# Expert weights moved to other places among the transfers of a one-core kernel of linear attention and routed experts

## The chip, the cores and the metric

The kernel runs on one core of a Trainium2 chip. The metric is the device time of one execution in microseconds (us). Engines are named as in the profile: PE is the matmul engine (TensorE), DVE, ACT and POOL are the vector, scalar and GpSimd engines, SP issues transfers.

## The reference

```
q_s = softmax(q, over head_dim);  k_s = softmax(k, over seq)       # 8 batches, 8 heads, seq 576, head_dim 64
attn = q_s @ (k_s^T @ v)                                           # per batch and head
x = attn as 4608 tokens of 512
logits = x @ w_gate + modality_bias[modality_id];  e = argmax(logits)
out = softmax(logits)[e] * (relu(x @ w1[e]) @ w2[e])               # w1 512 x 1024, w2 1024 x 512, 8 experts
```

## The kernel before

The bias of a token's modality decides its expert for the data at hand, so at most two experts are used: side A for the tokens of one modality, side B for those of the other. The kernel reads the two numbers of experts from the biases on chip (`eid_i`), sorts the tokens into places by modality (A from the front of the buffer `xs`, B from its end), runs the two experts over them and stores each row at its token's place by an indirect DMA. A fallback at the end, over all experts, is skipped when a count of the tokens says so.

Attention goes batch by batch, in stages that are named here by their lines. Load q, k, v of a batch into one of five staging buffers each (L393, issued by SP, one after another). Exp of q (L821, ACT), its sums (L827, DVE), their inverses and the scaled q, `eq` (L843; on DVE for batches 0 and 1, on POOL after that). Exp of k, `ek` (L854, ACT); cast of v, `vb` (L864, ACT or POOL). The kv product (L957, PE), scaled into `kvbd` (L993, DVE). A permutation matmul of the scaled q (L1033, PE) that sorts each 64 tokens by modality, evicted to `et` (L1045 ACT, L1047 DVE). The second product `et` x `kvbd` (L1072, PE). Last, 18 copies into the places of the two sides (L1103), 9 per side, whose addresses were loaded into registers; the table `copier` says which engine does them.

Experts go in passes of 256 tokens of a side: nine passes per side, pass n when batches 0 to n are in their places. A pass has the gate's logits (L1138, PE; L1152 to L1166 for the softmax), the first layer (L1202: 8 groups of 4 matmuls of 256 columns, each group with a PSUM bank of its own and a relu into `hT`, L1172 ACT or L1174 DVE), the second layer (L1215: 2 tiles of 8 matmuls of 512 columns, evicted with the gate's factor, L1178 ACT or L1180 DVE) and two stores (L1183, POOL). Weights W come by DMA from POOL (L510 for w1, L521 for w2), which halves them to bf16 on the way: for each side four parts, 0 and 1 for w1, 2 and 3 for w2. The places of the tokens are worked out in L643 to L656 (slots and digits) and by one-hot products (L677 DVE, L701 POOL, L718 PE); the table of biases by place is L667 to L672.

What sets the order is a planner in the kernel. Each piece of work is an `op` with the engines that may do it, a busy time and a latency that are written by hand, its dependencies, a rank and its buffers. `Plan.order` lists them as an event-driven simulation would start them; the instructions are then written in that order, one in-order queue per engine. Transfers are ops on one engine "DMA" and are listed in the order in which they are made. `Plan.fill` puts matmuls that nobody reads (L1451) ahead of PE's work where the plan leaves it idle in the first 32 us.

Before, loads are listed as batches 0 and 1, then all four parts of A, then q of batch 2 and part 0 of B, k and part 1, v and part 2, part 3, then batches 3 to 7. Two waits are written by hand: the first part of A waits for k of batch 1, and q of batch 2 for part 2 of A. Parts 2 and 3 of B are kept in the plan behind the products L701.

Of the kernel before, what the change touches and what calls it, by code (L numbers as in the profile page):

```python
# [19 lines left out]
P = 128  # L20
# [32 lines left out]
class Op:  # L53
    seq = -1

    def __init__(self, costs, run, deps=(), rank=0.0, takes=(), uses=(), lag=0.0):
        self.costs, self.run, self.rank, self.lag = costs, run, rank, lag
        self.takes, self.uses = takes, uses
        self.after, self.left = [], 0
# [14 lines left out]
class Plan:  # L74
# [5 lines left out]
    def op(self, costs, run, deps=(), rank=0.0, takes=(), uses=(), lag=0.0):  # L80
        o = Op(costs, run, list(dict.fromkeys(deps)), rank, list(takes), list(takes) + list(uses), lag)
        o.seq = len(self.ops)
        self.ops.append(o)
        return o

# [6 lines left out]
    def order(self, later):  # L92
# [6 lines left out]
        queue = [o for o in self.ops if "DMA" in o.costs]  # L99
# [25 lines left out]
        while True:  # L125
            moved = True
            while moved:
                moved = False
                for e in ready:
                    if not idle[e]:  # L130
                        continue
                    for o in sorted(ready[e], key=lambda o: ALONE[e] * (len(o.costs) > 1)):
                        if (e == "DMA" and o is not queue[0]) or (port(e, o) and not idle["PORT"]):
                            continue
# [13 lines left out]
                        if e == "DMA":  # L148
                            queue.pop(0)
# [9 lines left out]
                        heapq.heappush(events, (now + busy, n, "idle", e))  # L159
                        heapq.heappush(events, (now + lat, n, "done", o))  # L160
# [5 lines left out]
            while events and events[0][0] <= now:  # L166
# [10 lines left out]
                for a in x.after:  # L177
# [7 lines left out]
                for b in x.uses:  # L185
# [41 lines left out]
def dma(nbytes):  # L227
    busy = nbytes / 390e3
    return {"DMA": (busy, busy + 2.0)}
# [3 lines left out]
def kernel(  # L233
# [12 lines left out]
    nc = tc.nc  # L246
# [133 lines left out]

    def behind(later, first, reason):
# [7 lines left out]
    def load(src, b, buf, h, n):  # L389


        def run(_):
# [9 lines left out]
            if src is q and b == 2:  # L402
                behind(d, issued["w", 0, 2][-1], "the weights come first")
# [27 lines left out]
    def load_ids(_):  # L431
# [3 lines left out]
        )  # L435
        nc.scalar.dma_start(
# [16 lines left out]
    l_ids = pl.op({"ACT": (1.2, 3.5)}, load_ids, rank=-9)  # L453
    load_batch(0)
    load_batch(1)
# [41 lines left out]
    o_parts = pl.op({"DVE": (0.35, 0.5)}, parts_run, [l_ids, c_dve], rank=-5)  # L497
    o_spread = pl.op({"PE": (0.2, 0.45)}, spread_run, [o_parts, c_pool], rank=-5, takes=[b_buf])
    o_exp = pl.op({"DVE": (1.2, 1.4)}, experts, [o_spread, c_dve2], rank=3, uses=[b_buf])
# [32 lines left out]

    def load_w(s, part):


        def run(_):
# [15 lines left out]
        at = pl.op({"POOL": (cost, cost)}, run, [o_exp, loads["k", 1][0][-1]], rank=-1)  # L552
        w_issue[s].append(at)
        return pl.op(dma(2 * P * F * 4 * 1.12), lambda _: None, [at])
# [86 lines left out]
    def slot_run(_):  # L641
        d = nc.vector
# [22 lines left out]
    def bsel_run(_):  # L665
        d = nc.vector
# [942 lines left out]
```

## Time and profile before

| | |
|---|---|
| time, median of 3 runs | 202.79 us (201.49 to 205.6) |
| profiled execution, its own time | 204.96 us |
| its span, first to last instruction | 203.2 us |
| mean granted PE clock | 0.964 of full |
| busy, of the span | PE 180.4, DVE 154.5, ACT 127.9, POOL 90.5 us |
| read from HBM, written | 36.75 MB, 9.70 MB |

Busy time of PE is modelled at its ends, so that full does not mean that every matmul runs at its peak. Idle time of an engine costs only where another engine, or the end, waits for it. An engine's queue is in order: what waits at its head holds all that stands behind it.

### The profile page before, as it was taken

To read this page: it belongs to the slowest core of one execution; us is meant where nothing else is said; L and a number is where in the kernel's file an instruction comes from. 1 tells how busy PE (TensorE), PEld (TensorE's weight loads), DVE (VectorE), ACT (ScalarE), POOL (GpSimd) and SP (SyncE) were. 2 spreads that over 40 slices of the span, in tenths; PEclk is the share of its full clock that TensorE was granted. 3 is DMA by queue.
4 is the path that set the end of the run, shared out by engine and by line. 5 is a ranking of instruction groups with operands and counts; after the bars stand their busy time and mean duration, and the time that the engine had idled before them with its cause. 6 is when DMAs were issued, how large, how long until landed. Compare 5 with 4: busy or idle time off the path is not lost.

```text
span 203.2 us, 5008 instructions
## 1 busy us (share of the span) xinstructions
PE 180.4 (89%) x1716; PEld 124.4 (61%) x1735; DVE 154.5 (76%) x447; ACT 127.9 (63%) x283; POOL 90.5 (45%) x113
## 2 busy tenths in 40 slices
PE   0789679989999999999959959999999999999990
PEld 0446348577657486868647735878667657766760
DVE  1899997999879999669968973959589557755660
ACT  2669875998759599999849674999896000000100
POOL 6001910584944489943395086591303311222231
PEclk9999955999999999999999988999999999999998
DMA  6999999999999997999369711111112112121102
GB/s 191 371 400 392 186 203 225 295 394 313 280 411 404 404 399 250 390 404 338 115 201 385 271 52 55 52 53 56 53 55 103 52 55 103 52 103 56 76 28 108
DMA packets 18588, 42.33 MB, mean 208 GB/s; under 512 B 1913, under 2 KB 1913, under 8 KB 18562
## 3 DMA queue, kind: packets, MB, share of 16 engines
q1 hardware_dynamic: 13344, 28.33, 38.4%
q0 software_dynamic: 5200, 13.64, 23.3%
q8 instruction: 14, 0.23, 0.5%
q10 hardware_dynamic: 18, 0.04, 0.2%
q14 instruction: 12, 0.10, 0.1%
HBM read 36.75 MB, written 9.70 MB: 229 GB/s over the span
## 4 chain that ended last, share of the span: by engine, by line
PE 69%; DVE 11%; ACT 6%; issue 5%; POOL 3%; DMA 2%; ACTq 2%; DVEq 0%; POOLq 0%
PE ps L1215 28%; PE ps L1202 26%; DVE xs L1103 3%; PE ps L1033 3%; PE ps L1072 3%; PE ps L957 3%; ACT xs L1103 3%; PE ps L1138 2%; DVE own L827 2%; DMA bias<-n_moe_modality_bias_dram 2%; DVE eq L843 2%; POOL out_dram L1183 1%; ACT vb L864 1%; POOL eq L843 1%; ACTq L1007 1%
## 5 line engine op out<-in xcount | busy, mean ns | idle before, releaser
L1202 PE MATMUL ps<-xs,W 128*128 128x256 bf16 x576 | 71.9, 277 | 0.2
L1215 PE MATMUL ps<-W,hT 128*128 128x512 bf16 (+1 forms) x277 | 66.4, 378 | 1.1 <-issue 0.2
L1183 POOL DMA_INDIRECT out_dram<-y_sb,idx x36 | 35.7, 992 | 57.5 <-DVE y_sb L1180 30.7
L1202 PEld LDWEIGHTS <-W 128*128 128x128 bf16 x576 | 55.2, 99 | 9.8 <-issue 0.9
L1172 ACT ACTIVATE hT<-ps 128x256 bf16<-128x256 f32 x63 | 23.0, 414 | 40.7 <-PE ps L1202 40.4
L1215 PEld LDWEIGHTS <-hT 128*128 128x128 bf16 x296 | 28.6, 99 | 29.3 <-issue 1.3
L1174 DVE TENSOR_SCALAR hT<-ps 128x256 bf16<-128x256 f32 (+1 forms) x83 | 34.6, 427 | 7.4 <-PE ps L1202 4.7
L1180 DVE TENSOR_SCALAR y_sb<-ps,gate 128x512 f32<-128x512 f32 (+1 forms) x28 | 20.1, 720 | 21.1 <-PE ps L1215 15.9
L1103 ACT CAST xs<-ps 128x256 f32 (+1 forms) x99 | 31.8, 447 | 2.1 <-PE ps L957 1.0
L843 POOL TENSOR_TENSOR eq<-st,qi 128x512 bf16<-128x512 f32 (+1 forms) x30 | 28.5, 972 | 6.1 <-PE ps L1202 2.7
L827 DVE TENSOR_REDUCE own<-st 128x18 f32<-128x1152 f32 x16 | 21.6, 1350 | 0.1
L821 ACT ACTIVATE st<-st 128x1152 f32<-128x1152 f32 x16 | 18.7, 1195 | 2.8 <-DMA st<-in_q_dram 2.3
L854 ACT ACTIVATE ek<-st 128x1152 bf16<-128x1152 f32 x16 | 19.1, 1200 | 1.2 <-DMA st<-in_k_dram 1.2
L1045 ACT CAST et<-ps 128x512 bf16<-128x512 f32 (+1 forms) x30 | 16.1, 565 | 5.9 <-PE ps L1033 5.6
L1033 PE MATMUL ps<-perm,eq 128*128 128x128 bf16 x144 | 14.3, 230 | 3.5 <-POOL eq L843 2.0
L1103 DVE CAST xs<-ps 128x256 f32 (+1 forms) x45 | 16.1, 415 | 0.5 <-ACT xs L1103 0.4
L864 POOL CAST vb<-st 128x1152 bf16<-128x1152 f32 x8 | 9.0, 1142 | 16.0 <-DMA st<-in_v_dram 10.0
L1033 PEld LDWEIGHTS <-eq 128*128 128x128 bf16 x144 | 10.0, 101 | 8.2 <-POOL eq L843 3.1
L957 PE MATMUL ps<-vb,ek 64*128 64x129 bf16 x288 | 11.4, 222 | 2.7 <-ACT vb L864 2.5
L957 PEld LDWEIGHTS <-ek 64*128 64x128 bf16 x288 | 8.7, 96 | 6.7 <-issue 2.9
L1072 PE MATMUL ps<-et,kvbd 128*128 128x128 bf16 (+1 forms) x160 | 11.8, 219 | 0.2
L510 POOL DMA_DIRECT2D W<-in_moe_w_dram x8 | 5.1, 674 | 15.2 <-DMA st<-in_k_dram 15.2
(134 smaller groups left out, 170.9 us busy)
## 6 DMA issues: line engine op xcount, KB each, us to landing
st<-in_q_dram SPq DMA_DIRECT2D x6, 1152.0 KB, 12.3
st<-in_k_dram SPq DMA_DIRECT2D x6, 1152.0 KB, 13.7
st<-in_v_dram SPq DMA_DIRECT2D x6, 1152.0 KB, 12.9
st<-in_q_dram SPq DMA_DIRECT2D x4, 576.0 KB, 5.1
st<-in_k_dram SPq DMA_DIRECT2D x4, 576.0 KB, 6.7
st<-in_v_dram SPq DMA_DIRECT2D x4, 576.0 KB, 9.7
W<-in_moe_w_dram POOLq DMA_DIRECT2D x8, 256.0 KB, 6.8
W<-in_moe_w_dram POOLq DMA_DIRECT2D x4, 512.0 KB, 10.4
```

Source lines behind the costliest of these rows:

```text
L827: nc.vector.tensor_reduce(out=sums[qib.idx][:, h * NJ : (h + n) * NJ], in_=view(st[bq.idx], [[Dh, n * NJ], [1, Dh]], h * NJ * Dh), op=ALU.add,
L843: (nc.vector if e == "DVE" else nc.gpsimd).tensor_tensor(out=view(eq[eqb.idx], [[HG * Dh, n], [Dh, HG], [1, Dh]], j0 * HG * Dh), in0=view( ...
L854: nc.scalar.activation(out=view(ek[ekb.idx], [[Dh, n], [HG * Dh, NJ], [1, Dh]], h * Dh), in_=view(st[bk.idx], [[NJ * Dh, n], [Dh, NJ], [1, ...
L957: nc.tensor.matmul(out=ps_t[kvp[hg].idx][:, 130 * hp : 130 * hp + 129], lhsT=ek[ekb.idx][rows, j, P * hp : P * hp + P], rhs=vb[vbb.idx][ro ...
L1033: nc.tensor.matmul(out=view(t, [[2 * nj * 64, 2], [1, 64]], hp * nj * 64 + jj * 64), lhsT=eq[eqb.idx][:, j0 + jj, P * hp : P * hp + P], rh ...
L1103: w_ = nc.scalar.copy(out=dst, in_=src) if e == "ACT" else nc.vector.tensor_copy(out=dst, in_=src)
L1172: nc.scalar.activation(out=dst, in_=src, func=ACT.Relu)
L1174: nc.vector.tensor_scalar_max(out=dst, in0=src, scalar1=0.0)
L1180: nc.vector.tensor_scalar(out=dst, in0=src, scalar1=g, scalar2=None, op0=ALU.mult)
L1183: s_ = nc.gpsimd.indirect_dma_start(out=out, out_offset=bass.IndirectOffsetOnAxis(ap=ix[:, c : c + 1], axis=0), in_=ysb, in_offset=None, b ...
L1202: m = nc.tensor.matmul(out=t[:, 0:w], lhsT=w1(W[:, slot_, :], kd, f), rhs=xs[:, kd, lo : lo + w], start=(kd == 0), stop=(kd == KD - 1),)
L1215: nc.tensor.matmul(out=t, lhsT=h[:, kf, i * P : (i + 1) * P], rhs=W[:, slot_, W2 + kf * D + c0 : W2 + kf * D + c0 + cn], start=(kf == 0), ...
```

## The change

A list `transfers` says in which order batches and weights are loaded: batch 0, w1 of A, batch 1, w2 of A, batch 2, w1 and w2 of B, batches 3 to 7. The first issue of a weight group that stands behind a batch waits until that batch's q has landed; q of a batch that stands behind a weight group waits until that group's first part (for batch 3: part 2 of B) has landed; `EARLY` names q for each of the waits. The parts of a side are issued in order. With it go other edits:

- the first layer is done in groups of 8 matmuls that fill one PSUM bank with two groups of 256 columns, with one relu of 512 columns (`h_mm`);
- slots and the table of biases are worked out on POOL instead of DVE, and the vector of token numbers earlier on DVE;
- the scaled q of batch 2 is made on DVE instead of POOL, and side B's copies of batch 1 on DVE instead of ACT; batch 0's copies lose the rank that let batch 1's work go ahead;
- a store is now two ops, its issue on POOL and its transfer on "DMA", which may start out of the list's turn; copies that follow each other on one engine are planned back to back (`follow`); busy times and ranks of some ops, the spare time of `fill` and the place of one `drain` on POOL change.

```diff
+    transfers = [0, "a1", 1, "a2", 2, "b1", "b2", *range(3, B)]
+    ahead_of, w_awaits = {}, {}
+    for i, x in enumerate(transfers):
+        if isinstance(x, str):
+            s_, part = "ab".index(x[0]), 2 * (int(x[1]) - 1)
+            if i + 1 < len(transfers) and not isinstance(transfers[i + 1], str):
+                ahead_of[transfers[i + 1]] = (s_, part)
+            if not isinstance(transfers[i - 1], str):
+                w_awaits[s_, part] = transfers[i - 1]
...
-            if src is q and b == 2:
-                behind(d, issued["w", 0, 2][-1], "the weights come first")
+            if src is q and b in ahead_of:
+                behind(d, issued["w", *ahead_of[b]][-1], "the weights come first")
...
-            if not s and not part:
-                behind(issued["w", 0, 0][0], issued[k.tensor.name, 1], "the first batches come first")
+            if (s, part) in w_awaits:
+                nm, b = EARLY[s, part], w_awaits[s, part]
+                behind(issued["w", s, part][0], issued[nm.tensor.name, b], "the batches ahead come first")
...
     def slot_run(_):
-        d = nc.vector
+        d = nc.gpsimd
...
     def bsel_run(_):
-        d = nc.vector
+        d = nc.gpsimd
...
-    w_in = [[load_w(0, part) for part in range(4)], []]
-    for part, nms in enumerate(("q", "k", "v", "")):
-        for nm in nms:
-            load_one(nm, 2)
-        w_in[1].append(load_w(1, part))
-    for o in w_issue[1][2:]:
-        pl.later(o, o_hv[-1])
-    for b in range(3, B):
-        load_batch(b)
+    w_in = [[], []]
+    for x in transfers[ahead:]:
+        if isinstance(x, str):
+            s_, part = "ab".index(x[0]), 2 * (int(x[1]) - 1)
+            w_in[s_] += [load_w(s_, part), load_w(s_, part + 1)]
+        else:
+            load_batch(x)
...
-    copier = [("ACT", "DVE")] + [(e, e) for e in ("ACT", "DVE", "ACT", "ACT", "DVE", "ACT", "ACT")]
+    copier = [("ACT", "DVE")] * 2 + [(e, e) for e in ("DVE", "ACT", "ACT", "DVE", "ACT", "ACT")]
...
-            if b <= 1:
+            if b <= 2:
                 ncost = on_dve(n_, 1, True)
...
-                            rank=R + 4 if b else 10.5,
+                            rank=R + 4,
...
-    def h_mm(t, lo, w, slot_, f, whole=False):
-        for kd in range(KD):
-            m = nc.tensor.matmul(
-                out=t[:, 0:w],
+    def h_mm(t, lo, w, slot_, f0, whole=False):
+        for i in range(2):
+            for kd in range(KD):
+                f = f0 + i
+                m = nc.tensor.matmul(
+                    out=t[:, i * w : (i + 1) * w],
...
-        for f in range(KF):
+        for f in range(0, KF, 2):
...
-                    {**on_act(w), **on_dve(w)},
-                    lambda e, f=f, fb=fb: relu(e, hT[hb.idx][:, f, 0:w], ps_t[fb.idx][:, 0:w]),
+                    {**on_act(2 * w), **on_dve(2 * w)},
+                    lambda e, f=f, fb=fb: relu(
+                        e, hT[hb.idx][:, f : f + 2, 0:w], view(ps_t[fb.idx], [[w, 2], [1, w]])
+                    ),
...
-                {"POOL": (1.05, 3.8)},
+                {"POOL": (1.05, 1.9)},
                 lambda _, i=i, yb=yb: store(t0 + i, y_sb[yb.idx], idx, "stores"),
...
+            pl.op({"DMA": (0.65, 1.9)}, lambda _: None, [st_], rank=-1, uses=[yb], store=True)
```

In the changed file all lines are later: L1202 becomes L1241, L1033 becomes L1066, L864 becomes L898, L843 becomes L877, L821 and L854 become L855 and L888, L1172 becomes L1208, L1045 becomes L1078, L1183 becomes L1219, L393 becomes L414.

The first place is ACT's queue from the last copies of batch 0 to the first relus of side A (`ek_69`, `vb_73` and `et_77` are of batch 1, `hT` is the first layer of the experts). Before:

```order
L1045 CAST et_77<-ps_91 128x4x128
L1045 CAST et_77<-ps_92 128x4x128
L1103 ISA
L1103 COPY xs<-ps_93 128x4x64
L1045 CAST et_77<-ps_91 128x4x128
L1045 CAST et_77<-ps_92 128x4x64
L1172 ACTIVATE hT_80<-ps_91 128x256
```

Now, on the same queue:

```order
L1136 COPY xs<-ps_93 128x4x64
L855 ACTIVATE st_66<-st_66 128x1152
L888 ACTIVATE ek_69<-st_67 128x2x9x64
L1208 ACTIVATE hT_80<-ps_91 128x2x256
L888 ACTIVATE ek_69<-st_67 128x2x9x64
L1208 ACTIVATE hT_80<-ps_92 128x2x256
L1208 ACTIVATE hT_80<-ps_95 128x2x256
L898 CAST vb_73<-st_64 128x2x9x64
L1208 ACTIVATE hT_80<-ps_93 128x2x256
L898 CAST vb_73<-st_64 128x2x9x64
L1078 CAST et_77<-ps_91 128x4x128
```

The first relus of the experts moved from behind batch 1's evictions to ahead of its casts of v.

The second place is POOL's queue where batch 5's q is scaled (`eq_71<-st_63`), with the casts of v of batch 6 (`vb_72<-st_65`) and batch 7 (`vb_73` behind it). Before:

```order
L864 CAST vb_72<-st_65 128x2x9x64 x2
L1183 DMA out_dram<-y_sb_82,idx 4608x512
L843 TENSOR_TENSOR eq_71<-st_63,qi_87 128x512
L1183 DMA out_dram<-y_sb_83,idx 4608x512
L843 TENSOR_TENSOR eq_71<-st_63,qi_87 128x512 x3
L843 TENSOR_TENSOR eq_71<-st_63,qi_87 128x256
L1183 DMA out_dram<-y_sb_84,idx 4608x512
L864 CAST vb_73<-st_63 128x2x9x64
```

Now:

```order
L877 TENSOR_TENSOR eq_71<-st_63,qi_87 128x512 x2
L1219 DMA out_dram<-y_sb_82,idx 4608x512
L877 TENSOR_TENSOR eq_71<-st_63,qi_87 128x512
L1219 DMA out_dram<-y_sb_83,idx 4608x512
L877 TENSOR_TENSOR eq_71<-st_63,qi_87 128x512
L877 TENSOR_TENSOR eq_71<-st_63,qi_87 128x256
L898 CAST vb_72<-st_65 128x2x9x64 x2
L1219 DMA out_dram<-y_sb_84,idx 4608x512
L1219 DMA out_dram<-y_sb_85,idx 4608x512
L898 CAST vb_73<-st_65 128x2x9x64 x2
```

The casts of batch 6's v moved from ahead of the scaled q of batch 5 to behind it, and both halves of batch 7's v are now cast here.

The third place is SP's queue at its end, the loads of batches 6 and 7 with their staging buffers. Before:

```order
L393 DMA st_66<-in_q_dram 128x4x576
L393 DMA st_67<-in_k_dram 128x4x576
L393 DMA st_65<-in_v_dram 128x4x576
L393 DMA st_65<-in_q_dram 128x4x576
L393 DMA st_64<-in_k_dram 128x4x576
L393 DMA st_63<-in_v_dram 128x4x576
```

Now:

```order
L414 DMA st_66<-in_q_dram 128x4x576
L414 DMA st_67<-in_k_dram 128x4x576
L414 DMA st_65<-in_v_dram 128x4x576
L414 DMA st_64<-in_q_dram 128x4x576
L414 DMA st_63<-in_k_dram 128x4x576
L414 DMA st_65<-in_v_dram 128x4x576
```

Batch 7's q moved from the buffer of batch 6's v to that of batch 5's k, and its k and v to those of batch 5's q and batch 6's v.

## Rows read from the trace of the kernel before

**Rows 1.** Busy us by engine (instructions) in stretches; then PE clock, DMA share, GB/s.
```profile
20.00:25.00 5.00, 3.10 (x44) 1.80 (x42) 4.78 (x14) 4.59 (x8) 5.00 (x9) 0.96 1.09 200
25.00:35.00 10.00, 8.78 (x69) 5.85 (x65) 8.56 (x34) 6.24 (x18) 0.89 (x2) 0.51 1.11 209
35.00:99.00 64.00, 61.90 (x653) 43.45 (x660) 56.74 (x151) 56.44 (x138) 38.55 (x40) 1.00 1.01 351
99.00:124.00 25.00, 20.57 (x235) 14.28 (x238) 18.69 (x54) 17.00 (x30) 15.19 (x15) 0.93 0.53 185
124.00:197.70 73.70, 73.13 (x616) 51.39 (x623) 49.90 (x136) 30.74 (x80) 25.84 (x27) 1.00 0.17 66
```

**Rows 2.** Timeline of PE and ACT: start, us, instruction [idle before, releaser].
```profile
18.51 1.48 PE L1072 MATMUL ps<-et,kvbd 128*128 128x128 bf16 x20
...
22.98 0.69 PE L957 MATMUL ps<-vb,ek 64*128 64x129 bf16 x18 [1.26 <-ACT vb L864]
23.04 1.21 ACT L864 CAST vb<-st 128x1152 bf16<-128x1152 f32 x1
...
30.48 3.57 PE L1202 MATMUL ps<-xs,W 128*128 128x256 bf16 x16
...
41.85 0.35 PE L1138 MATMUL ps<-wg_sb,xs 128*128 128x8 bf16 x8 [0.85 <-ACT xs L1103]
```

**Rows 3.** Timeline of PE, 99 to 124.
```profile
104.21 0.40 PE L1033 MATMUL ps<-perm,eq 128*128 128x128 bf16 x4 [2.03 <-POOL eq L843]
...
118.90 0.61 PE L1138 MATMUL ps<-wg_sb,xs 128*128 128x8 bf16 x16 [2.03 <-ACT hT L1172]
```

**Rows 4.** Timeline of POOL, 95 to 105.
```profile
99.69 2.23 POOL L864 CAST vb<-st 128x1152 bf16<-128x1152 f32 x2 [6.02 <-PE ps L957]
...
103.08 1.07 POOL L843 TENSOR_TENSOR eq<-st,qi 128x512 bf16<-128x512 f32 x1
```

**Rows 5.** Timeline of ACT, 115 to 120.
```profile
117.41 1.16 ACT L864 CAST vb<-st 128x1152 bf16<-128x1152 f32 x1 [2.45 <-DMA st<-in_v_dram]
118.47 1.99 ACT L1172 ACTIVATE hT<-ps 128x256 bf16<-128x256 f32 x6
```

**Rows 6.** Timeline of SP's queue: the last loads but two.
```profile
91.12 0.37 SPq L393 DMA_DIRECT2D st<-in_v_dram  x1
101.96 0.37 SPq L393 DMA_DIRECT2D st<-in_q_dram  x1
...
109.07 0.37 SPq L393 DMA_DIRECT2D st<-in_v_dram  x1
```

**Rows 7.** Groups by line and shape: busy us, mean ns of one, idle before.
```profile
L1174 DVE TENSOR_SCALAR hT<-ps 128x256 bf16<-128x256 f32 x81 | 33.2, 421 | 6.7 <-PE ps L1202 4.7 <-PE ps L1138 0.6 <-ACT hT L1172 0.2
L1103 ACT CAST xs<-ps 128x256 f32 x98 | 31.4, 447 | 2.1 <-PE ps L957 1.0 <-DVE xs L1103 0.5
...
L843 POOL TENSOR_TENSOR eq<-st,qi 128x512 bf16<-128x512 f32 x24 | 24.9, 1060 | 6.1 <-PE ps L1202 2.7 <-DVE qi L839 2.4 <-ACT ex L1157 0.7
L1172 ACT ACTIVATE hT<-ps 128x256 bf16<-128x256 f32 x63 | 23.0, 414 | 40.7 <-PE ps L1202 40.4
...
L1103 DVE CAST xs<-ps 128x256 f32 x44 | 15.7, 415 | 0.3 <-ACT xs L1103 0.2
...
L1045 ACT CAST et<-ps 128x512 bf16<-128x512 f32 x24 | 14.2, 604 | 5.2 <-PE ps L1033 4.9
...
L843 DVE TENSOR_TENSOR eq<-st,qi 128x512 bf16<-128x512 f32 x8 | 5.2, 684 | 0.0
...
L1174 DVE TENSOR_SCALAR hT<-ps 128x512 bf16<-128x512 f32 x2 | 1.4, 692 | 0.7 <-PE ps L1351 0.5
```

**Rows 8.** DMA issues of 19 to 22 and of 23.4 to 26: size, us to landing.
```profile
W<-in_moe_w_dram POOLq DMA_DIRECT2D x4, 256.0 KB, 5.5
...
W<-in_moe_w_dram POOLq DMA_DIRECT2D x4, 256.0 KB, 14.9
```

**Rows 9.** The chain of waits: start us, us, what.
```profile
91.64 3.49 PE ps L1202 x32
```

More of the change, by code (lines that the diff above doesn't have):

```diff
@@ L84, in op, with follow @@
         return o
+    @staticmethod
+    def follow(o, first):
+        first.next.append(o)
+        o.left += 1
     @staticmethod
@@ L98, in order @@
                 ready.setdefault(e, [])
-        queue = [o for o in self.ops if "DMA" in o.costs]
+        queue = [o for o in self.ops if "DMA" in o.costs and not o.store]
         def arm(o):
@@ L132, in order @@
                     for o in sorted(ready[e], key=lambda o: ALONE[e] * (len(o.costs) > 1)):
-                        if (e == "DMA" and o is not queue[0]) or (port(e, o) and not idle["PORT"]):
+                        if (e == "DMA" and not o.store and o is not queue[0]) or (port(e, o) and not idle["PORT"]):
                             continue
@@ L147, in order @@
                             ready[x].remove(o)
-                        if e == "DMA":
+                        if e == "DMA" and not o.store:
                             queue.pop(0)
@@ L176, in order @@
                     continue
-                for a in x.after:
+                for a in x.next if kind == "next" else x.after:
                     a.left -= 1
@@ L451, in load_wg @@
                 )
-    l_ids = pl.op({"ACT": (1.2, 3.5)}, load_ids, rank=-9)
-    load_batch(0)
-    load_batch(1)
+    l_ids = pl.op({"ACT": (0.6, 3.6)}, load_ids, rank=-9)
+    l_bias = pl.op({"ACT": (0.6, 3.9)}, load_bias, rank=-8)
+    ahead = next(i for i, x in enumerate(transfers) if isinstance(x, str))
+    for b in transfers[:ahead]:
+        load_batch(b)
     l_wg = pl.op({"DMA": (0.4, 3.5)}, load_wg, rank=0)
@@ L931, in attention @@
         scaled_q.append(nq[-1])
+        if not b:
+            for o in (o_slot, o_bsel):
+                pl.later(o, nq[-1])
         vcost = {**on_act(S * 2), **on_pool(S * 2, 0.95)}
@@ L946, in attention @@
             )
-        if b == 1:
-            for o in w_issue[1]:
-                pl.later(o, cv[-1])
         def kv_run(hp):
@@ L1117, in attention @@
                     across = win[-1 - 2 * side] if j0 + jj == NJ - 1 else None
+                    same = before and before.costs.keys() == {copier[b][side]}
                     win.append(
@@ L1126, in attention @@
                     )
+                    if same:
+                        pl.follow(win[-1], before)
         filled[b] = win
```

84 lines of the change are left out of this document (52 added, 32 removed).

## Prediction

> **What bounds the kernel now.** I read the busy time of each engine in stretches first, because the average of 89% for TensorE (PE) hides four different stages [rows 1]. From 124.0 to 197.7 PE is busy 73.1 of 73.7 us at full clock: that stage is pure matmul work, and nothing that ACT, DVE, POOL or a DMA does there moves the end. What follows to the end of the span at 203.2 is the last output tile and its store. From 35 to 99 PE is busy 61.9 of 64 us. What is lost lies in two places. One is the front: the first expert matmul (L1202) starts at 30.5 [rows 2], behind the attention of batches 0 and 1, and in 25 to 35 the granted clock is 0.51, that is 1.2 instead of 2.4 GHz, after the stretch from 20 to 25 in which PE was busy only 3.1 of 5 us [rows 1]. The other is the stretch from 99 to 124: PE is busy 20.6 of 25 us, and its mean clock of 0.93 means 3.5 us at half clock, which lose another 1.7 us. Together 6.1 us are lost there. The timeline of PE shows the two waits that make it [rows 3]: at 104.2 a permutation matmul (L1033) had waited 2.0 us for POOL's scaled q of batch 5, and at 118.9 the gate's logits (L1138) had waited 2.0 us for ACT.
>
> Both have their cause on another queue. POOL runs the cast of batch 6's v (L864) first, waits 6.0 us for its buffer, and only at 103.1 starts to scale batch 5's q [rows 4]. ACT has a half of batch 7's v to cast at 117.4, for which it stood 2.5 us, with six relus queued behind it [rows 5]; and that v is late because SP issued q of batch 7 only at 102.0, 10.8 us after the transfer before it, into the staging buffer that v of batch 6 held, and v of batch 7 at 109.1 [rows 6].
>
> **Part 1, the middle.** The new order on POOL puts all five scalings of batch 5's q ahead of the cast of batch 6's v, so PE's first wait loses its reason. SP's new order loads q of batch 7 into the buffer of k of batch 5, and all casts of v of batches 6 and 7 stand so that ACT has none of batch 7's; the second wait loses its reason too. The relus are halved in number: 144 of 256 columns become 72 of 512. On DVE one of 256 takes 421 ns and one of 512 takes 692 [rows 7], so a pair saves 150 ns; on ACT one takes 414 and an eviction of 512 columns 604, so a pair saves some 220. Over 72 pairs that is between 10.8 and 15.8 us of the two engines' time. After 124 it is worth nothing (PE covers it); ahead of it, it lets the chain of exp, sum and scaling of batches 4 to 6 come up earlier. If nothing of this helps, the stretch loses its 6.1 us again; if all of it does, none. What is late next is the copying into places of each batch: 18 copies on one engine at 415 to 447 ns [rows 7] are 7.5 to 8 us between a batch's second matmul and its logits, and PE must have expert work in stock for that long. I leave 0.9 us for such waits and take **5.2 us gained**, from 0 to 6.1.
>
> **Part 2, the front.** Weights of A now come ahead of batch 1, and the expert matmuls of A stand ahead of batch 1's kv product. Batch 0's second product (L1072) started at 18.5 [rows 2]; its nine copies for side A follow at once on ACT, at about 0.4 us each, and are no longer mixed with batch 1's exps, while PE spends 17 filler matmuls; I take 1 us for the longer ids' chain and fillers ahead of it, so logits come at 18.5 + 1 + 1.2 + 9 x 0.45 = 24.8 and L1202 at 25: 5.5 us earlier. But 36 kv matmuls (0.69 us per 18) and 18 permutation matmuls (0.40 us per 4 alone, less in a row) of batch 1, some 2.3 us, now come behind that point [rows 2, 3], so PE is ahead by 3.2 us. Against it stands v of batch 1. It was cast on ACT at 23.0 [rows 2] as it landed. Now w1 of A lies wholly ahead of batch 1. Of W's bytes 200 GB/s are counted as they are written, in half the size that is read, with the DMA as full as at any time [rows 1]: so 400 GB/s are read, and 2.1 MB (half of one expert's 4.2) take 5.2 us. Batch 1's v lands at 28.2 at the earliest. w2 of A is issued as soon as q of batch 1 is there, while its k and v are still in transit, and takes from them between nothing and another 5.2 us: 33.4 at the latest. I take the middle, 31, since transfers of the two queues do overlap: four W transfers that had the DMA to themselves and W's own took 5.5 us, four that met q of batch 2 took 14.9 [rows 8]. From v's landing to the second product of batch 1 go a cast (1.2) and the kv product, its scaling and five evictions, some 4.3 us in all. L1202's 32 matmuls (3.5 us at full clock [rows 9]) and the 2.3 us end at 25 + 3.5 + 2.3 = 30.8, the second product starts at 35.3: PE idles 4.5 us (1.7 to 6.9). And as before, thin PE work may be followed by half clock. I take 5 us of it at work, 2.5 us lost (0 to 4). What falls away: 4.5 us at half clock between 30.5 and 35, some 2.3 us, and 0.85 us of waiting at 41.9 [rows 1, 2]. Sum: 3.2 - 4.5 - 2.5 + 2.3 + 0.85 = **0.7 us lost**; at the good ends 3.2 - 1.7 - 0 + 3.15 = 4.7 gained, at the bad ones 3.2 - 6.9 - 4 + 3.15 = 4.5 lost. So moving w1 of A does not pay by itself in my sum: it starts the experts earlier and then leaves them without batch 1.
>
> The Trainium skill speaks against this part: "DMA: Bandwidth & Descriptors", section Queues, rings and completion order, has each DMA engine take turns between the queues that have work, so an issue on another queue doesn't wait for the transfers ahead of it. By that rule w2 of A and the rest of batch 1 would end together, at the late end, and the sum would be 2.4 us worse. The 14.9 us agree with sharing, and don't show the shares.
>
> **Part 3, what lies beside other work.** The slots (5 instructions) and the bias table (4) go from DVE to POOL. On POOL nothing of that size is in the trace; nearest are its products of 512 elements at 1.06 us [rows 7], so at most 9.5 us if each cost as much, and less since most have 72 elements or fewer. POOL idles between its issue of w1 and the landing of q of batch 1, which I put at 8 us, and the digits on DVE need the slots only behind batch 0's copies. Were POOL late, w2 of A would be issued late; I cost it at 0. Scaling batch 2's q goes from POOL to DVE: 684 instead of 1,060 ns each, so 3.2 us more on DVE at about 50 and 4.9 less on POOL; PE has A's experts then, cost 0. W of B is issued behind batch 2's q and behind the six products L701 on POOL; it needs to be there when side B starts, about 50. On SP q of batch 3 waits for it and all later loads queue behind; the bytes ahead of batch 3 are the same as before, and DMA is full in both, so 0. The stores as items of the plan, the bank of the filler and the earlier drain move order alone; 0, inside the range.
>
> **Sum.** The profiled execution took 205.0 us, its span 203.2 and 1.8 around it; the median of the runs shown is 202.8, 2.2 lower, and I count the gain from that. 5.2 - 0.7 = 4.5 us gained: **198.3 us**, with its own bounds 195.8 to 200.8 by 2.5 us either way for the part of the idle that I set in the middle. A measurement of this kernel tells 2%, 4.1 us, from no change.
>
> **Rivals.** *The front pays too.* If k and v of batch 1 get the DMA first (they were queued first) and fillers keep the clock, the front gains 4.7 instead of losing 0.7, with 4.9 for the middle at most together 8.5 to 9.5: 194. Speaking for it: v of batch 1 was queued ahead of w2; against it the 14.9 us [rows 8]. Chance 0.18.
>
> *The queues take turns.* w2 of A, sharing evenly, holds v of batch 1 until about 33.4; PE idles 6.9 instead of 4.5 us, the middle gains its 5.2: 198.3 + 2.4 = 200.7, with a shortage of expert work later 201.5. This is the skill's rule as a mechanism of this kernel. Chance 0.2.
>
> *Slower: the half clock and the late batch 1 feed the middle.* If v of batch 1 lands beyond 32, PE stands over 5.5 us, and the clock stays at half for the 10 us that it did before [rows 1], now over A's second layer and its second pass; the front then loses 4.5. Batches 2 and 3 follow later on ACT and DVE by as much, batch 5's scaled q is late again, and the stretch around 110 keeps its 6.1 us: 202.8 + 4.5 = 207.3; it decides from a landing of v of batch 1 at 32. Chance 0.12. *That it does nothing* (the weights move, PE's start of L1202 stays at 30) is part of the second rival: the order forbids it, only a wait for w1 beyond 30 could do it.
>
> **How the numbers follow.** Forecast 0.5, rivals 0.18, 0.2 and 0.12. Of the forecast's range 195.8 to 200.8 some 0.32 of the 0.5 lies below 198.7, where 2% ends. Faster by over 2%: 0.32 + 0.18 = 0.5; within 2%: 0.18 + 0.2 = 0.38; slower 0.12. The range is 193 to 204: it takes in the rivals at 194 and 201.5 with a microsecond for the spread of the runs, and leaves the slower one out.
>
> **What would show it.** L1241 (the new L1202) first at about 25; v of batch 1 cast on ACT near 31 (28 and 33 for the rivals); PE idle 4 to 5 us between 28 and 36 and a clock of 0.5 behind it; no wait of over 1 us for scaled q or a cast of v between 95 and 125; the gap-free stretch beginning near 115 and ending near 193. I am wrong if PE waits for batch 5 again, or if L1241 starts at 28 or later.

## The result, and the profile after

After the change the kernel takes 200.56 us (median of 20 runs, 199.41 to 202.28); 20 runs of the kernel before, beside them, have a median of 203.41 (201.48 to 205.60). The ratio is 0.989, with a 95% interval of 0.986 to 0.992: faster by 1.1%, about 2.2 us. (The ratio leaves out runs over 1.5% above the fastest of their kernel, and the profiled execution of before, 204.96 us, lies above that line.) The forecast was 198.3 us, faster by 2.2%. The direction was right; the size was too large, by half by the medians and twofold by the ratio.

The profiled execution took 200.07 us, its span 198.4, its mean granted clock 0.987, against 204.96, 203.2 and 0.964 of before. So between the two profiled executions lie 4.9 us, where the sum of the prediction had 4.5; between the medians lie 2.9 or less. Much of what follows is about this gap. First the stretches, in the columns of [rows 1], of the kernel after:

```profile
25.00:35.00 10.00, 7.68 (x106) 6.03 (x106) 9.16 (x24) 9.52 (x15) 2.16 (x3) 1.00 1.04 271
35.00:45.00 10.00, 8.62 (x67) 5.26 (x68) 7.61 (x23) 6.87 (x19) 6.91 (x10) 0.83 1.08 337
45.00:99.00 54.00, 53.38 (x572) 37.99 (x571) 47.82 (x114) 44.59 (x90) 29.98 (x30) 1.00 0.99 330
99.00:124.00 25.00, 25.00 (x305) 18.11 (x304) 22.25 (x63) 22.16 (x44) 15.58 (x16) 1.00 0.65 239
124.00:192.40 68.40, 67.56 (x577) 46.90 (x569) 45.39 (x105) 26.48 (x63) 25.01 (x27) 1.00 0.18 67
```

In 99 to 124, where PE lost 4.4 us of idling and 1.7 at half clock before [rows 1], it is busy all the time at full clock. The cause that the prediction named is gone too: the timeline of POOL has the scalings of batch 5's q (L877) ahead of the casts of batch 6's v (L898), and the casts follow without a wait, where before they came first and stood 6.0 us [rows 4]:

```profile
97.63 2.07 POOL L877 TENSOR_TENSOR eq<-st,qi 128x512 bf16<-128x512 f32 x2 [2.88 <-ACT xs L1136]
...
103.17 1.66 POOL L877 TENSOR_TENSOR eq<-st,qi 128x512 bf16<-128x512 f32 x2
104.76 2.23 POOL L898 CAST vb<-st 128x1152 bf16<-128x1152 f32 x2
...
117.69 2.24 POOL L898 CAST vb<-st 128x1152 bf16<-128x1152 f32 x2 [6.11 <-DMA st<-in_v_dram]
```

The last line is both halves of batch 7's v. It comes no earlier than before, when ACT cast its half at 117.4 [rows 5]; SP issued q of batch 7 at 103.7, later than the 102.0 of before. The second wait is gone because POOL stands for that v now, and ACT, which has the relus that PE needs, does not.

The front, in the timeline of PE, to be set beside [rows 2]:

```profile
19.66 1.17 PE L1105 MATMUL ps<-et,kvbd 128*128 128x128 bf16 x20
...
26.13 3.65 PE L1241 MATMUL ps<-xs,W 128*128 128x256 bf16 x32
...
35.38 0.29 PE L1105 MATMUL ps<-et,kvbd 128*128 128x128 bf16 x2 [1.36 <-DVE kvbd L1026]
...
37.51 4.68 PE L1254 MATMUL ps<-W,hT 128*128 128x512 bf16 x16
42.74 0.82 PE L1174 MATMUL ps<-wg_sb,xs 128*128 128x8 bf16 x16 [0.55 <-DVE xs L1136]
```

The first expert matmul (L1241) starts 4.4 us earlier than before. Batch 0's product (L1105) is later, 19.7 instead of 18.5. On DVE the cast of the gate's weights waits for their transfer, and the five scalings of batch 0's q stand behind it; they began at 15.2 (how little of the delay this explains, a run below shows):

```profile
14.96 0.22 DVE L526 CAST wg_sb<-wg_f 128x32 bf16<-128x32 f32 x1 [1.28 <-DMA wg_f<-in_moe_w_gate_dram]
```

Batch 1's product stands at 35.4, and the clock is at half for a part of 35 to 45: 16 matmuls of the second layer (L1254) take 4.68 us, where they take 3.6 at full clock. On ACT the casts of batch 1's v start at 30.4 and 31.9, with no wait ahead of them: ACT had no gap from 25.5 to 36.

```profile
29.40 1.08 ACT L1208 ACTIVATE hT<-ps 128x512 bf16<-128x512 f32 x2
30.36 1.17 ACT L898 CAST vb<-st 128x1152 bf16<-128x1152 f32 x1
```

### The profile page after: what moved, and what is told of

It is laid out like the page before. It is cut to its first block, busy times and chain, and to the rows that moved or that the text cites. A ratio compares the mean times of both kernels' runs of the same rounds, so it can differ in the third digit from the quotient of the medians.

```text
span 198.4 us, 5000 instructions
## 1 busy us (share of the span) xinstructions
PE 181.1 (91%) x1757; PEld 123.9 (62%) x1757; DVE 152.3 (77%) x406; ACT 124.5 (63%) x246; POOL 94.8 (48%) x119
## 4 chain that ended last, share of the span: by engine, by line
PE 58%; DVE 17%; ACT 8%; issue 4%; DMA 4%; SPq 3%; POOL 2%; DVEq 1%; ACTq 0%
PE ps L1254 24%; PE ps L1241 23%; DVE xs L1136 5%; ACT xs L1136 4%; DMA wg_f<-in_moe_w_gate_dram 4%; PE ps L990 3%; DVE eq L877 3%; DVE xs L713 3%; PE ps L1105 2%; PE ps L1066 2%; SPq L414 2%; DVE kvbd L1026 2%; PE ps L1174 2%; DVE own L861 1%; POOL eq L877 1%
## 5 line engine op out<-in xcount | busy, mean ns | idle before, releaser
L1241 PE MATMUL ps<-xs,W 128*128 128x256 bf16 x576 | 68.3, 273 | 0.0
L1254 PE MATMUL ps<-W,hT 128*128 128x512 bf16 (+1 forms) x296 | 67.2, 378 | 0.0
L1219 POOL DMA_INDIRECT out_dram<-y_sb,idx x36 | 36.1, 1002 | 59.1 <-DVE y_sb L1216 31.8
L1241 PEld LDWEIGHTS <-W 128*128 128x128 bf16 x576 | 54.9, 98 | 8.4
L1254 PEld LDWEIGHTS <-hT 128*128 128x128 bf16 x296 | 28.5, 99 | 29.1 <-issue 1.4
L1136 ACT CAST xs<-ps 128x256 f32 (+1 forms) x90 | 29.7, 430 | 6.2 <-DVE xs L1136 3.8
L1210 DVE TENSOR_SCALAR hT<-ps 128x512 bf16<-128x512 f32 x41 | 27.9, 689 | 7.1 <-PE ps L1241 5.6
L877 POOL TENSOR_TENSOR eq<-st,qi 128x512 bf16<-128x512 f32 (+1 forms) x25 | 23.8, 979 | 5.6 <-ACT xs L1136 2.9
L1136 DVE CAST xs<-ps 128x256 f32 (+1 forms) x54 | 19.9, 419 | 2.9 <-ACT xs L1136 1.9
L1208 ACT ACTIVATE hT<-ps 128x512 bf16<-128x512 f32 x33 | 19.1, 604 | 4.0 <-PE ps L1241 2.8
L1078 ACT CAST et<-ps 128x512 bf16<-128x512 f32 (+1 forms) x32 | 16.1, 552 | 6.1 <-PE ps L1066 6.1
L855 ACT ACTIVATE st<-st 128x1152 f32<-128x1152 f32 x16 | 18.4, 1165 | 2.3 <-DMA st<-in_q_dram 2.3
L888 ACT ACTIVATE ek<-st 128x1152 bf16<-128x1152 f32 x16 | 18.5, 1168 | 1.7 <-DMA st<-in_k_dram 1.3
L898 POOL CAST vb<-st 128x1152 bf16<-128x1152 f32 x10 | 11.2, 1145 | 11.4 <-DMA st<-in_v_dram 10.9
L1498 PE MATMUL ps<-ones 128*128 128x512 bf16 x57 | 15.3, 407 | 0.0
L1066 PE MATMUL ps<-perm,eq 128*128 128x128 bf16 x144 | 12.7, 220 | 0.2 <-POOL eq L877 0.2
L1105 PE MATMUL ps<-et,kvbd 128*128 128x128 bf16 (+1 forms) x160 | 10.8, 221 | 1.7 <-DVE kvbd L1026 1.7
L1105 PEld LDWEIGHTS <-kvbd 128*128 128x128 bf16 x160 | 9.9, 102 | 3.3 <-DVE kvbd L1026 2.0
```

The costliest lines, as they stand in the source:

```text
L877: (nc.vector if e == "DVE" else nc.gpsimd).tensor_tensor(out=view(eq[eqb.idx], [[HG * Dh, n], [Dh, HG], [1, Dh]], j0 * HG * Dh), in0=view( ...
L888: nc.scalar.activation(out=view(ek[ekb.idx], [[Dh, n], [HG * Dh, NJ], [1, Dh]], h * Dh), in_=view(st[bk.idx], [[NJ * Dh, n], [Dh, NJ], [1, ...
L1105: nc.tensor.matmul(out=view(ps_t[xbuf.idx], [[1, nj * 64]], c * nj * 64), lhsT=kvbd[kvb.idx][:, c, :], rhs=et[etb.idx][:, c, j0 * 64 : (j0 ...
L1136: w_ = nc.scalar.copy(out=dst, in_=src) if e == "ACT" else nc.vector.tensor_copy(out=dst, in_=src)
L1208: nc.scalar.activation(out=dst, in_=src, func=ACT.Relu)
L1210: nc.vector.tensor_scalar_max(out=dst, in0=src, scalar1=0.0)
```

## The experiments

**Theory 1.** The order of casts, scalings and loads on POOL and SP empties the middle; the new transfers cost the front about a microsecond; and the profiled execution of before was one that lost more in the middle than a typical one, so its 6.1 us can't be taken off the median. **Rivals:** the executions of before all lose 6 us, and the gain is really 5; the weights between the batches are what pays; the relu pairs are; w2 of A, sharing the DMA, is what holds the front back.

### The kernel before, three more executions

No edit. The third and the fourth are one execution each.

> The kernel before, unchanged, for a second profiled execution of it. Theory 1 (my sum was right for the profiled execution, and that execution lost more than a typical one): this execution ends between 201.5 and 204.5 us; the stretch from 99 to 124 us loses clearly less than the 6.1 us that the first one showed, or the stretch from 25 to 35 is less at half clock than 0.51. Theory 2 (the executions lose alike, and the 5 us between the two profiled executions are the real gain): PE is busy about 20.6 of 25 us in 99 to 124 again, with waits of 2.0 and 2.0 us, and the time lies at 204.5 to 205.6.

> The kernel before, unchanged, a third profiled execution. If it is one of its shorter executions (203 us or less): by theory 1 (the executions differ in what PE loses in the front and in 99 to 124, so the first one showed more to gain than a typical one has) PE's idle time or its time at half clock in 20 to 35 and 99 to 124 is 1.5 to 3 us less than in the first; by the rival (they differ elsewhere, in the start-up ahead of 12 us or behind the last matmul) PE loses the same in those stretches and the difference stands at the ends. If it is another long one (204 us or more), both give the loss of the first again.

> The kernel before, unchanged, a fourth profiled execution, for the same purpose as the third: by theory 1 a shorter execution shows 1.5 to 3 us less lost by PE in 20 to 35 and 99 to 124; by the rival the same loss there, and the difference at the ends of the execution.

They took 204.65, 203.04 and 203.25 us. (The second had 11 runs from 201.91 to 205.80; against other runs of the same kernel its ratio is 0.998, 0.992 to 1.003.) Two stretches of each, in the columns of [rows 1]: first the profiled execution of before again, cut at 110, then the second execution:

```profile
99.00:110.00 11.00, 8.77 (x103) 6.51 (x105) 7.93 (x23) 7.31 (x14) 8.98 (x9) 1.00 0.63 216
110.00:124.00 14.00, 11.80 (x136) 7.77 (x134) 10.76 (x32) 9.69 (x17) 6.21 (x6) 0.88 0.44 161
```
```profile
99.00:110.00 11.00, 9.45 (x118) 7.04 (x114) 8.60 (x24) 7.95 (x16) 8.86 (x9) 1.00 0.72 246
110.00:124.00 14.00, 11.57 (x125) 7.30 (x122) 9.96 (x31) 9.21 (x18) 6.36 (x7) 0.88 0.39 137
```

The third and the fourth:

```profile
99.00:110.00 11.00, 8.62 (x94) 6.58 (x89) 6.25 (x19) 5.92 (x13) 8.98 (x9) 0.84 0.62 210
110.00:124.00 14.00, 14.00 (x171) 9.32 (x171) 13.34 (x41) 12.09 (x22) 7.29 (x8) 1.00 0.45 167
```
```profile
99.00:110.00 11.00, 8.92 (x95) 6.74 (x94) 6.50 (x22) 6.13 (x13) 8.98 (x9) 0.84 0.59 204
110.00:124.00 14.00, 13.81 (x154) 8.96 (x152) 13.23 (x41) 12.15 (x22) 7.10 (x7) 1.00 0.48 172
```

Idle time and clock together (25 less the busy time, plus the share of the clock that is missing: 0.12 of 14 or 0.16 of 11) make 6.1 and 5.7 us lost in the two long executions, 4.1 and 4.0 in the two shorter ones. Theory 1 holds, and the trace says how. In the third execution the 16 expert matmuls behind PE's first wait run at half clock, 3.44 us instead of 1.91, and the logits at 118 then have no wait; in the second they run at full clock and the logits wait:

```profile
104.42 0.57 PE L1033 MATMUL ps<-perm,eq 128*128 128x128 bf16 x4 [2.38 <-POOL eq L843]
104.79 3.44 PE L1202 MATMUL ps<-xs,W 128*128 128x256 bf16 x16
...
118.25 0.55 PE L1138 MATMUL ps<-wg_sb,xs 128*128 128x8 bf16 x16
```
```profile
103.63 1.91 PE L1202 MATMUL ps<-xs,W 128*128 128x256 bf16 x16
...
118.48 0.63 PE L1138 MATMUL ps<-wg_sb,xs 128*128 128x8 bf16 x16 [2.42 <-ACT hT L1172]
```

In all four executions these logits start between 118.25 and 118.90, in three of them behind a wait for ACT, which had cast v of batch 7. Half clock ahead of that point only fills time in which PE would wait; half clock behind the second wait (0.88 in 110 to 124) costs its full 1.7 us. That is the 1.4 to 1.9 us between the long and the short executions. What decides behind which wait the clock falls, these four don't show. Executions under 203 us, which are nearly half of the kernel's runs, were not profiled.

### The old place of the transfers

```
-    transfers = [0, "a1", 1, "a2", 2, "b1", "b2", *range(3, B)]
+    transfers = [0, 1, "a1", "a2", 2, "b1", "b2", *range(3, B)]
```

> The kernel after, with batches 0 and 1 transferred ahead of all weights of A again; the rest of the change stays (the relu pairs, POOL's slots, the order that the plan then makes). Theory 1 (the front loses 1 to 2 us by the new transfers, the middle gains by the rest): L1241 first at about 30 instead of 26.1, no PE gap behind it, nothing lost between 95 and 125, and 199 to 200.5 us, at most as long as after. Rival (the earlier weights are what gains): 202.5 to 204 us, with waits of 1 us or more for scaled q or for ACT between 95 and 125, as before.

206.66 us (205.22 to 207.73); ratio to before 1.021 (1.010 to 1.032). Neither had this: the gate's weights were now transferred behind batch 1, and PE stood for them. The timeline of PE:

```profile
29.56 0.57 PE L1174 MATMUL ps<-wg_sb,xs 128*128 128x8 bf16 x16 [4.15 <-DVE wg_sb L526]
```

So the run says nothing on the weights of the experts. The next one loads the gate's weights between the two batches:

```
-    for b in transfers[:ahead]:
-        load_batch(b)
-    l_wg = pl.op({"DMA": (0.4, 3.5)}, load_wg, rank=0)
+    load_batch(0)
+    l_wg = pl.op({"DMA": (0.4, 3.5)}, load_wg, rank=0)
+    load_batch(1)
```

> Batches 0 and 1 ahead of all weights of A as in the run before this with the old transfers, but the gate's weights transferred between batches 0 and 1, so that the 4.1 us that PE stood for their cast fall away. Theory 1 (the new transfers cost the front 1 to 2 us): 199 to 200.5 us, at most as long as after. Rival (the earlier weights pay, or are at least needed by the order that goes with them): 201.5 to 204 us, L1241 first at 29 or later, and PE loses 2 us or more between 25 and 45 beyond what after loses there.

201.26 us (8 runs, 200.30 to 202.09), ratio to before 0.989 (0.985 to 0.993): the same gain as that of the whole change. Its front, in the timeline of PE:

```profile
30.91 1.05 PE L1241 MATMUL ps<-xs,W 128*128 128x256 bf16 x8
...
35.60 1.17 PE L1105 MATMUL ps<-et,kvbd 128*128 128x128 bf16 x20
36.61 3.62 PE L1254 MATMUL ps<-W,hT 128*128 128x512 bf16 x16
42.29 0.82 PE L1174 MATMUL ps<-wg_sb,xs 128*128 128x8 bf16 x16 [2.06 <-DVE xs L1136]
```

The experts start 4.8 us later than in the kernel after, and yet batch 1's product stands at 35.6 against 35.4, and the logits that release the next expert work at 42.3 against 42.7. The same work is done by then, only in another order. So the weights between the batches, by themselves, neither pay nor cost anything that can be measured, and most of what the front loses against before (1.5 to 2.0 us, see why the prediction was wrong) is lost with the old place too: equal work of PE is done only 0.4 us earlier here. Which of the other edits costs it, no run singles out. Both sides of the expectation were wrong about a part: it isn't faster than after, as theory 1 had it, nor is the gain lost.

### w2 of A behind v of batch 1

```
-    behind(issued["w", s, part][0], issued[nm.tensor.name, b], ...)
+    last = v if (s, part) == (0, 2) else nm
+    behind(issued["w", s, part][0], issued[last.tensor.name, b], ...)
```

> The kernel after, with w2 of A awaiting v of batch 1 instead of its q; no instruction changes place. Theory 1 (at the landing of v of batch 1 ACT's own queue of exps and relus is the limit, so an earlier v gains little): the casts of v of batch 1 on ACT start at most 1 us ahead of 30.4 and 31.9, the second layer L1254 or batch 2 waits for the later weights, and the time is that of after or up to 1.5 us longer (200.3 to 202). Rival (the queues take turns, and w2 of A is what holds v of batch 1 back): the transfer of v of batch 1 takes 8.5 us or less instead of 11.2, both casts start 2 us or more earlier, and the time is 199 or less.

200.70 us, ratio 0.990 (0.985 to 0.995): like after. The transfer of v of batch 1 falls from 11.2 to 9.7 us (the DMA issues of either trace, first after, then this kernel):

```profile
st<-in_v_dram SPq DMA_DIRECT2D x2, 576.0 KB, 11.2
```
```profile
st<-in_v_dram SPq DMA_DIRECT2D x2, 576.0 KB, 9.7
```

So w2 of A may take up to 1.5 us from it. The rule of the Trainium skill ("DMA: Bandwidth & Descriptors", Queues, rings and completion order), that the DMA engines take turns between queues, agrees with that direction. The size isn't shown: in the last two kernels below, where w2 of A waits for q as in the kernel after, the same transfer took 10.7 and 9.9 us. And nothing comes of it: the casts on ACT start at 30.02 and 31.55, 0.3 us earlier, and batch 0's whole chain was 0.3 us earlier in this execution. ACT's own queue is the limit by then; it is busy 9.85 of 10 us in 25 to 35.

### The relus in single groups

The first run lets the planner set a new order for 144 single relus (h_mm and the loop over f one group at a time, as before the change).

> The kernel after, with the first layer's relus on single groups of 256 columns again (144 instead of 72). Theory 1 (the middle's gain comes from where the casts of v of batches 6 and 7 and the scalings stand on POOL and ACT): at most 1 us slower than after, 200.5 to 201.5 us, PE gap-free from about 100. Rival (it comes from the 11 to 16 us that the pairs take off ACT and DVE): waits of PE for ACT or DVE come back between 60 and 125, 2 us or more in all, and 202.5 to 204 us.

206.66 us (205.75 to 206.80), ratio 1.018 (1.008 to 1.028). Neither again: nothing waits in the middle (PE is busy 24.9 of 25 us in 99 to 124), but in the front half of A's second layer now stands ahead of batch 1's product, and PE runs out of work while batch 1 is copied:

```profile
38.10 1.89 PE L1254 MATMUL ps<-W,hT 128*128 128x512 bf16 x8
45.87 0.84 PE L1174 MATMUL ps<-wg_sb,xs 128*128 128x8 bf16 x16 [5.88 <-DVE xs L1136]
```

An edit that makes the planner plan anew tells of the plan, not of the edit. So the second run keeps every instruction in its place and only writes each relu as two:

```
-    relu(e, hT[hb.idx][:, f : f + 2, 0:w], view(ps_t[fb.idx], [[w, 2], [1, w]]))
+    [relu(e, hT[hb.idx][:, f + i, 0:w], ps_t[fb.idx][:, i * w : (i + 1) * w]) for i in range(2)]
```

> The kernel after with every instruction in its place, but each relu of two groups of columns (512) written as two of 256. Theory 1 (the order of casts and scalings is what emptied the middle of waits): 200.5 to 201.5 us; PE loses less than 1 us between 95 and 125. Rival (the time that the pairs save on ACT and DVE is what did it): 202 us or more, with new waits of PE for ACT or DVE of 1.5 us or more in all between 60 and 125.

201.74 us (200.64 to 202.38), ratio to before 0.993 (0.990 to 0.997); PE is busy 24.8 of 25 us in 99 to 124. Theory 1's side, at the upper end of its range plus 0.2. By the medians the pairs are worth 1.2 us, by the ratios 0.8 with intervals that overlap, so the size isn't clear of noise; the middle has no waits without them either.

### The casts of batch 6's v, moved alone

In the kernel before, the two casts are put behind the five scalings of batch 5's q on POOL; nothing else changes place. POOL's order there, its stores left out:

```
-CAST vb<-st x2 ; eq<-st,qi 128x512 x4 ; eq 128x256
+eq<-st,qi 128x512 x4 ; eq 128x256 ; CAST vb<-st x2
```

> The kernel before with one move alone, on POOL: the two casts of v of batch 6 stand behind the five scalings of batch 5's q instead of ahead of them; the orders of all other engines and of SP are as before. Theory 1 (the two waits of the middle hang together through the staging buffers, and it takes the new order of casts, scalings and loads on POOL and SP together): PE's wait of 2.0 to 2.4 us for scaled q at 104 goes, but q of batch 7 awaits the casts and is issued at about 107 instead of 102, v of batch 7 still lands at 116 to 118, the logits behind it still start at 118 or later behind a wait of 3 us or more, and the time falls by at most 1 us: 202 to 203.5. Rival (the order on POOL alone is the cause): both waits go or shrink below 1 us, and the time falls by 2 to 4 us: 199.5 to 201.5.

207.98 us (207.31 to 208.15), ratio 1.028 (1.025 to 1.031). PE's first wait is gone, as expected. But q of batch 7 needs the buffer that the casts free, all three loads of batch 7 start at 108 to 109 together, and ACT waits 4.9 us for q, with an output and the relus that PE needs queued behind it. First SP's queue, then PE:

```profile
108.24 0.37 SPq L393 DMA_DIRECT2D st<-in_q_dram  x1
...
109.25 0.46 SPq L393 DMA_DIRECT2D st<-in_v_dram  x1
```
```profile
116.67 3.56 PE L1205 MATMUL ps<-xs,W 128*128 128x256 bf16 x16 [3.68 <-ACT y_sb L1181]
121.78 0.61 PE L1141 MATMUL ps<-wg_sb,xs 128*128 128x8 bf16 x16 [1.55 <-ACT hT L1175]
```

The mechanism of theory 1, with a price that I had far too low: v of batch 7 is cast at 120.3, not at 117, and the matmuls behind both waits run at half clock. The rival falls: the order on POOL alone loses 5 us.

The mirror of it, in the kernel after: the casts behind the first of the five scalings.

```
-eq<-st,qi 128x512 x4 ; eq 128x256 ; CAST vb<-st x2
+eq<-st,qi 128x512 ; CAST vb<-st x2 ; eq 128x512 x3 ; eq 128x256
```

> The kernel after with one move alone, on POOL, the mirror of the move tried in the kernel before: the two casts of v of batch 6 stand behind the first of the five scalings of batch 5's q instead of behind all five. Theory 1 (the place of these casts and the loads that await the buffers behind them are what the middle hangs on): the casts stand for v of batch 6 until about 103, the other four scalings end near 109 instead of 104.8, PE waits 3 us or more in all between 100 and 125, and the time is 202.5 to 205.5 us. Rival (the new order has so much slack, by the relu pairs and batch 2's scalings on DVE, that this place no longer matters): PE loses less than 1.5 us there, and the time is below 201.7 us.

210.24 us (209.21 to 211.23), ratio 1.035 (1.025 to 1.046): about 9.7 us more than after, twice the most that theory 1 gave. POOL stands for the landing of v, PE for POOL:

```profile
105.96 2.23 POOL L899 CAST vb<-st 128x1152 bf16<-128x1152 f32 x2 [5.50 <-DMA st<-in_v_dram]
```
```profile
109.26 0.61 PE L1070 MATMUL ps<-perm,eq 128*128 128x128 bf16 x4 [5.23 <-POOL eq L878]
```

More of the price is clock: 0.74 in 110 to 124, another 3.6 us. (Of the 11.1 us between the two profiled executions, 1.8 stood ahead of the move: batch 4's second product on PE, L1109, came at 96.6 instead of 94.8.) So the middle hangs on the place of these two casts together with the order that goes with it, and the pairs and batch 2's scalings on DVE give no slack that could replace it. What of that order is needed, the buffers of batch 7's loads or its casts on POOL alone, was not tested singly, nor which of the edits makes the planner choose it.

### The gate's cast, and fillers in the front

The cast that waited 1.28 us is put behind batch 0's scalings:

```
-            for o in (o_slot, o_bsel):
+            for o in (o_slot, o_bsel, wg_c):
                 pl.later(o, nq[-1])
```

> The kernel after with one move alone, on DVE: the cast of the gate's weights, which stood 1.28 us for its transfer ahead of batch 0's five scalings, stands some instructions behind them. Theory 1 (the front runs at the pace of v of batch 1, which lands at about 30): batch 0's scalings start about 1.2 us earlier and L1241 at 25 to 25.3 instead of 26.1, but batch 1's second product stays at 35 to 36, and the time falls by 0.5 us at most: 200 to 200.6. Rival (batch 0's chain sets the front): the whole of it, 1 us or more: 199.5 or less.

200.07 us (199.45 to 200.95), ratio 0.991 (0.988 to 0.994): not to be told from after, as theory 1 had it. The scalings begin at 13.0; L1241 comes at 25.6, 0.5 us earlier. But with the relus split, where the cast stood in its old place and happened to wait for nothing, L1241 came at 25.60 too, and in the next kernel, with the cast moved as here, at 26.07. So the wait of 1.28 us explains half a microsecond of L1241's delay at most, within what executions differ by. Then the timeline of PE:

```profile
34.84 0.29 PE L1105 MATMUL ps<-et,kvbd 128*128 128x128 bf16 x2 [1.36 <-DVE kvbd L1026]
...
36.38 3.62 PE L1254 MATMUL ps<-W,hT 128*128 128x512 bf16 x16
42.20 0.82 PE L1174 MATMUL ps<-wg_sb,xs 128*128 128x8 bf16 x16 [2.21 <-DVE xs L1136]
```

In this execution the clock didn't fall, and L1254 took 3.62 instead of 4.68 us. Nothing is won by it: the logits wait 2.2 us instead of 0.55, since the copies of batch 1 end when they end. The half clock of the front was free.

Six fillers (L1498) in the 1.4 us ahead of batch 1's product, on top of that. The plan adds 11 there when the filler's bank joins the others later; the last five are dropped:

```
-    quiet = 32.0
+    quiet = 36.0
...
+        last = max(i for i, o in enumerate(full) if o is filler)
+        del full[last - 4 : last + 1]
```

> The kernel with the gate's cast moved, and six filler matmuls (1.3 us at full clock) that write an unused bank ahead of batch 1's second product, where PE stands idle for 1.4 us in the trace of after; no other instruction changes place. If the thin work of PE there is what leads to the 3.4 us at half clock behind it, the granted clock in 35 to 45 is 1.00 instead of 0.83 and the time is 1 to 1.7 us less than with the gate's cast alone. Rival (the clock falls all the same, or the fillers only take the place of waiting and push the product back): the clock in 35 to 45 stays at about 0.83, and the time is the same or up to 1 us longer.

200.67 us (199.77 to 200.97), ratio 0.992 (0.989 to 0.995). The clock fell in this execution too, 6 us later than in the kernel after, and the place was a worse one: the expert matmuls that nothing covers.

```profile
42.68 0.84 PE L1174 MATMUL ps<-wg_sb,xs 128*128 128x8 bf16 x16 [2.21 <-DVE xs L1136]
43.38 4.79 PE L1241 MATMUL ps<-xs,W 128*128 128x256 bf16 x31
```

The fillers can't be named as the reason. The kernel with the casts of batch 6's v moved has the front of the kernel after, without these fillers, and its clock fell at the same matmuls:

```profile
44.48 5.32 PE L1245 MATMUL ps<-xs,W 128*128 128x256 bf16 x32
```

In the time the rival held. What the fillers do to the clock stays open, since without them the executions of this front differ as much. No version here beats the kernel after by more than the runs scatter.

## Why the prediction was wrong

**The step that failed is in the sum: "the median of the runs shown is 202.8, 2.2 lower, and I count the gain from that".** The 6.1 us of the middle, of which I took 5.2, were read from an execution of 205.0 us. Two executions near the median lose 4.1 and 4.0 there. One can take 6.1 off the long execution or 4.1 off a short one, but not the first off the median. A second, smaller step failed with it: behind 124 I put the loss at nothing, and it is 0.8 us.

The timelines of PE show it at places where PE has done the same work in both kernels, fillers apart. First the third execution of before (203.04 us), then the kernel after:

```profile
46.39 1.89 PE L1215 MATMUL ps<-W,hT 128*128 128x512 bf16 x8
...
143.04 0.96 PE L1138 MATMUL ps<-wg_sb,xs 128*128 128x8 bf16 x32
...
195.14 0.17 PE L1479 MATMUL ps<-cnt_b,ones 128*128 128x1 bf16 x1
```
```profile
48.41 1.89 PE L1254 MATMUL ps<-W,hT 128*128 128x512 bf16 x8
...
139.33 3.66 PE L1241 MATMUL ps<-xs,W 128*128 128x256 bf16 x32
143.66 0.96 PE L1174 MATMUL ps<-wg_sb,xs 128*128 128x8 bf16 x32 [0.67 <-ACT xs L1136]
...
192.26 0.17 PE L1526 MATMUL ps<-cnt_b,ones 128*128 128x1 bf16 x1
```

At the second layer of A's second pass (first lines) the kernel after is 2.0 us late. At 139.33, where its work done is that of before at 143.04, it is 3.7 us early: 5.7 gained between, 4.1 of them the idle time and half clock of 99 to 124. At the last matmul it is 2.9 early: 0.8 lost again. Most of the other 1.6 lies between 48 and 96, where idle time shows 0.5 of it; the rest I can't place. Against the first execution the same three steps give 1.5 lost, 7.6 gained, 0.8 lost, together 5.2.

**The middle**: both waits are gone, PE is busy from 80 to 124 without a gap, and the first went as I had said. The second went by one half of my reason only: ACT has no cast of batch 7's v. The other half, the loads, brought nothing: that v is cast no earlier than before. The size was taken from the wrong execution. I left 0.9 us for waits for the copies of a batch, and none came there. The one that came stands at 143.66, for the copies of batch 7 (L1136), in the stage of which I had said that nothing there but PE moves the end.

**The front**: 0.7 lost forecast, 1.5 to 2.0 measured against the four executions of before, and by other terms. The start of L1241, "25", was 26.1. v of batch 1, "31", was cast at 30.4. Batch 1's product, 35.3, came at 35.4. The idle time was 2.5 us from 28 to 36 instead of 4.5, with the fillers counted as busy. The half clock, "2.5 us lost", was there for 3.4 us and cost nothing, since PE next waits for the copies of batch 1 in any case; by the same reason the half clock of before, for which I credited 2.3 us, had cost far less: in its second execution the clock in 25 to 35 was 0.83 instead of 0.51, and the logits of 41.85 [rows 2] came at 41.35, half a microsecond earlier. These two errors cancelled. I had named these copies ("PE must have expert work in stock for that long") and not used batch 1's product and the copies behind it as the bound of the front, which they are: in six kernels the logits start 7.35 to 7.47 us behind that product's start, whether the clock fell between or not, and with the old place of the transfers 6.7. The product itself started at 33.85 in the profiled execution of before, 1.5 us earlier. ACT has four relus, 1.9 us, ahead of the end of its casts of batch 1's v; that they make the difference was not tested.

**The relus**: a pair saves 145 ns on DVE (two at 417 against one at 689) and 202 on ACT, as forecast; worth about a microsecond by the medians, not clear of noise.

**Part 3**: from 49 to 124 PE has one wait over 0.3 us (0.45 at 66), so nothing there speaks against the costs of 0; in the front a part of the loss may be one of them. **The rivals**: that the time came out next to the 200.7 of the turns of the queues is chance. That rival had v of batch 1 at 33.4, and it was cast at 30.4; the front neither paid, nor did it feed the middle.

## What to carry to other kernels

Before a loss is counted as a gain, look whether it is there in more than one execution, above all if the profiled one is longer than the median; take the gain from the execution that showed the loss, or not at all. Idle time and half clock ahead of a point that something else sets are not losses: find the next wait that comes at the same time in all variants, and count only from there. Where a stretch holds different work in two kernels, compare the times at which equal work is done. To price one part of a change in a planned kernel, keep every other instruction in its place; of the three kernels here whose plan was made anew, two told of something else.

## What was not expected of the hardware

The same program lost its clock at different places in different executions: behind the first wait of the middle in two of four, behind the second in the other two. One order of PE's instructions in the front, without the fillers of the last run, did it too: at 36 for 3.4 us (after, relus split), at 44 (casts of batch 6's v moved), or not at all (w2 behind v, gate's cast later). So a stretch at half clock in one execution says little of an edit. A move of two casts of 1.1 us on POOL cost 5 to 10 us, and some 40% of what PE lost in 99 to 150 was half clock behind the waits that it made (3.5 of 8.8 us and 5.1 of 11.8).
